# Attention beside a spectral filter: a clamped integer tile read directly as the first phase term, and the shifted copies of every second key block of VectorE made on GpSimd

## The chip, the cores and the metric

The kernel runs on one core of one Trainium2 chip. The time is device microseconds (us) of one launch; the times before are 455.18 and 456.29 us, median 455.74. The engines appear as PE (TensorE, matrix products; PEld is its weight load), ACT (ScalarE, activation functions), DVE (VectorE), POOL (GpSimd) and SP (its queue issues the DMAs here). SBUF is the on-chip memory, PSUM the memory that PE writes.

## The reference

Two branches over x of 2048 x 448 (bf16) are mixed by a gate for each row:

```python
g = sigmoid((x * gate_w).sum(-1, keepdims=True))
q, k, v = split(x @ wqkv)                 # 16 heads of 28
p = softmax(q @ k.T * 28 ** -0.5)         # 2048 x 2048 per head
a = concat(p @ v) @ wo
b = irfft2(rfft2(x) * (w_r + 1j * w_i))   # over both axes
out = g * a + (1 - g) * b
```

## The kernel before

**Attention.** Heads are worked in four groups g of four (index s), the queries in four blocks c of 512; a pair (g, c) is a *query group* n, 16 in all. Keys are cut in 16 blocks kt of 128. For one (n, kt, s), a *unit*, PE makes a 128 x 512 score tile. Most units are exponentiated by ACT: a *step* takes three units (PSUM tile psA) or two (psB) in turn, one activation at L1081 writes them to a ring in SBUF, and PE multiplies them with the values into the PSUM tile pvb (PV below). There are 363 steps.

**The key blocks of VectorE.** `ND` gives 29 (n, kt) blocks to DVE instead: key block 15 and key block 14 of n = 1 to 14, and block 15 of n = 15. I number them 0 to 28 in this order, so the blocks of kt = 15 are even and those of kt = 14 odd. For each, PE makes four score tiles (a "dunit" each, into one of two PSUM tiles bg0 and bg1). DVE turns each into a 16-bit integer that, read as a bf16, is a coarse power of two (L1040, "first pass", tile y4). Four shifted versions of that integer (phases f = 0 to 3) are made from it by four further DVE instructions of 128 x 2048 (L1050, tile pd), and PE adds the four in PV with weights vd that hold a gain for each phase (made on POOL at L951). The four together are a smoother exponential than one. The pd tiles go round a ring of NPD = 6, the y4 tiles a ring of two.

**Background.** Projections, the spectral branch (L1257 to L1389), normalisation (L1178 to L1193) and output tiles (L1214) use the same bg0 and bg1: PE fills one, DVE empties it.

**What sets the order.** `Sched.run` plans all work with assumed durations (0.61 us for a DVE pass, and so on), due times and dependencies, and emits each engine's instructions in the planned order; `pin` keeps that order. On the chip every engine runs its queue strictly in order and waits on semaphores for what its next instruction needs: data from another engine, or a tile that is still read. A wrong assumed duration is not corrected on the chip.

POOL otherwise makes memsets at the start, copies of weights, the vd tiles (L951) and sixteen small casts of softmax weights into the value tiles (L895).

Of the kernel before, what the change touches and what calls it, by code (L numbers as in the profile page):

```python
# [14 lines left out]
U16 = mybir.dt.uint16  # L15
ACT = mybir.ActivationFunctionType
ALU = mybir.AluOpType
# [3 lines left out]
NT, J, P = 16, 8, 128  # L21
FS, FN = (0, 112), 113
LN2 = math.log(2.0)
UNITS = 512.0
SQ = math.sqrt(UNITS * (DH ** -0.5) / LN2)
PHASE = (0, 129, 258, 387)
PHGAIN = [2.0 ** (-d / UNITS) / (4 * 1.0406815) for d in PHASE]
NPD, DKT = 6, 3


def free_dims(ap, dims, offset=0):
# [372 lines left out]
class Kernel:  # L404
# [28 lines left out]
    def alloc(self):  # L433
        nc, tc, ctx = self.nc, self.tc, self.ctx
        per = ctx.enter_context(tc.tile_pool(name="per", bufs=1))
        ps = ctx.enter_context(tc.tile_pool(name="ps", bufs=1, space=bass.MemoryType.PSUM))
        self.psA = ps.tile([P, 3, 512], F32, name="psA")
        self.psB = ps.tile([P, 2, 512], F32, name="psB")
        self.pv = ps.tile([P, 512], F32, name="pvb")
        self.bgt = [ps.tile([P, 512], F32, name=f"bg{i}") for i in range(2)]  # L440
        T = lambda shape, dt, name: per.tile(shape, dt, name=name)
        self.cst = T([P, CSTN], BF16, "cst")
        self.zero = T([P, 256], BF16, "zero")
        self.xtok = T([P, NT, 450], BF16, "xtok")
        self.xT = [T([P, 4, 512], BF16, f"xT{b}") for b in range(4)]
        self.wpad = {}
        for g in range(4):
            for w in "qk":
                self.wpad[w, g] = T([P, 4, P], BF16, f"wp{w}{g}") if g < 3 else self.wpad[w, 0]
        self.wv0 = T([P, 4, 112], BF16, "wv0")  # L450
        self.wvr = T([P, 4, 337], BF16, "wvr")
        self.WV0 = {1: 0, 2: 113, 3: 225}
        self.wo_pad = [T([P, D], BF16, f"wo{g}") for g in range(4)]
        self.q = [T([P, S], BF16, f"q{g}") for g in range(4)]
        self.k = [T([P, S], BF16, f"k{g}") for g in range(2)] * 2
        self.vw = [T([P, NT, 4, 32], BF16, f"vw{g}") for g in range(2)] * 2
        self.w = [T([P, NT, 4], F32, f"w{g}") for g in range(4)]
        self.ring = T([P, self.RING, 512], BF16, "ring")
        self.sq = T([P, S], BF16, "sq")
        self.nrow = [T([16, 512], BF16, f"nrow{i}") for i in range(2)]  # L460
        self.pvs = [T([P, 512], F32, f"pvs{i}") for i in range(2)]
        self.rs = [T([P, 16], F32, f"rs{i}") for i in range(2)]
        self.rr = [T([P, 16], F32, f"rr{i}") for i in range(2)]
        self.rhl = [T([P, 2, 16], BF16, f"rhl{i}") for i in range(2)]
        self.r8 = [T([8, 512], BF16, f"r8{i}") for i in range(2)]
        self.y4 = [T([P, 4, 512], U16, f"y4{i}") for i in range(2)]
        self.pd = [T([P, 4, 512], BF16, f"pd{i}") for i in range(NPD)]
        self.vd = T([P, 4, DKT, 4, 32], BF16, "vd")
        self.vf = T([P, DKT, 4, DH + 1], F32, "vf")
        self.glog = T([P, NT], F32, "glog")  # L470
        self.ge = T([P, NT], F32, "ge")
        self.gs = T([P, NT], F32, "gs")
        self.og = T([P, NT], F32, "og")
        self.Bd = T([P, 4, F2], BF16, "Bd")
        self.R = T([P, 4, 256], BF16, "R")
        self.Binv = self.Bd
        self.X1 = T([P, NT, F2], BF16, "X1")
        self.U = T([P, 2, 2, NT, 128], BF16, "U")
        self.CSt = [T([P, 3, P], BF16, f"CS{i}") for i in range(2)]
        self.Wg = [T([P, 3, F], BF16, f"Wg{i}") for i in range(2)]  # L480
        self.RBt = [T([P, 2, 2 * P], BF16, f"RB{i}") for i in range(2)]
        self.UT = [T([P, 2, F], BF16, f"UT{i}") for i in range(2)]
        self.t12 = [T([P, 2, F], BF16, f"t12{i}") for i in range(2)]
        self.t34 = [T([P, 2, F], BF16, f"t34{i}") for i in range(2)]
        self.ZT = [T([P, 2, 256], BF16, f"ZT{i}") for i in range(2)]
        self.bm = self.xtok
        self.fin = [T([P, D], BF16, f"fin{i}") for i in range(2)]

        self.wraw0 = {w: 2 * 4 * 336 + 448 * i for i, w in enumerate("qk")}
# [479 lines left out]
    def attention(self):  # L969
        nc, sc = self.nc, self.sc  # L970
# [5 lines left out]
        for b in range(4):  # L976
            due = ts[0] + 4 * b * rate
# [29 lines left out]
            el[-1:-1] = ph  # L1007
            self.elems.append(el)
        self.pdops, self.pv_last = {}, {}
        pdseq, quadl = [], []  # L1010
        di = 0
        dlist = [(n, kt) for n in range(16) for kt in self.dk[n]]
        for n, kt in dlist:
            g, c = self.groups[n]
            el = self.elems[n]
            fdue = []
            for f in range(4):
                i = el.index(("d", kt, f))
                t = self.tstart[n]
                for e in el[:i]:  # L1020
                    if e[0] == "a":
                        t = max(t, self.T[self.unit_step[n, e[1], 3]])
                fdue.append(t + 1.0)
            rel = fdue[0] - 60.0
            ys = self.y4[di % 2]
            prevy = quadl[di - 2][1][-1] if di >= 2 else None
            p1s = []
            for s in range(4):
                it = Item()

                def fm(s=s, g=g, c=c, kt=kt, it=it):
                    self.mm(self.bgi(it), self.k[g][32 * s:32 * s + 32, 128 * kt:128 * kt + 128],
                            self.q[g][32 * s:32 * s + 32, 512 * c:512 * c + 512], True, True, tile_position=(32 * s, 0))
                due = fdue[0] - DUE_P + 0.6 * s
                m = sc.op("PE", 0.22, fm, self.kev[g, kt // 4] + self.qev[g, c], due - 1, rel, "row", it, name="dunit")
                m.n = s
                self.dunit_ops.append(m)

                def f1(s=s, it=it, ys=ys):
                    self.pin(nc.vector.tensor_scalar(out=ys[:, s, :], in0=self.bgi(it), scalar1=127 * UNITS,  # L1040
                                                     scalar2=0.0, op0=ALU.add, op1=ALU.max))
                p1s.append(self.dve(0.61, f1, [m, prevy], due, free=it, name="dp1"))
            phs = []
            for f in range(4):
                j = len(pdseq)
                pds = self.pd[j % NPD]

                def g1(ys=ys, pds=pds, f=f):
                    fl = lambda t: t[:].rearrange("p a b -> p (a b)")
                    self.pin(nc.vector.tensor_scalar(out=fl(pds).bitcast(U16), in0=fl(ys), scalar1=float(PHASE[f]),  # L1050
                                                     scalar2=0.25, op0=ALU.add, op1=ALU.mult))
                o = self.dve(0.61, g1, p1s + phs[-1:], fdue[f], name="dexp")
                phs.append(o)
                pdseq.append((o, n, kt, f))
                self.pdops[n, kt, f] = (o, pds, j)
            quadl.append((p1s, phs))
            di += 1

# [4 lines left out]
        for i, st in enumerate(self.steps):  # L1063
            slot = self.psA if len(st) and i % 2 == 0 else self.psB
            deps = [exps[i - 2]] if i >= 2 else []
            for (n, kt, s) in st:
                g, c = self.groups[n]
# [8 lines left out]
            m = sc.op("PE", 0.23, fm, deps, -1000 + i * .001, 0.0, "row", name="score")  # L1076
# [6 lines left out]
            e = self.act(0.052 + 512 * len(st) / 1200.0, fe, [m] + exps[-1:], i * .001, name="exp")  # L1083
# [9 lines left out]
        pd_reader = {}  # L1093
# [3 lines left out]
        for n, (g, c) in enumerate(self.groups):  # L1097
            quads = self.elems[n]
            pairs = [quads[i:i + 2] for i in range(0, len(quads), 2)]
            for pi, pair in enumerate(pairs):  # L1100
                deps = [prev_pv]
# [3 lines left out]
                for kind, kt, *f in pair:  # L1105
                    deps += self.vready[g, kt // 4]
                    if kind == "a":
                        for s in range(4):
                            deps.append(unit_exp[n, kt, s])
                        tk = max(tk, self.T[self.unit_step[n, kt, 3]])  # L1110
                    else:
                        deps += [self.pdops[n, kt, f[0]][0], self.vdready[g]]

                def fm(pair=pair, pi=pi, n=n, g=g, last=(pi == len(pairs) - 1)):
                    for qi, (kind, kt, *f) in enumerate(pair):
# [8 lines left out]
                o = self.pe(0, fm, deps, tk + 2.0, mode="col", name="pv", dur=0.225 * len(pair))  # L1124
# [13 lines left out]
        for e in exps:  # L1138
            for ug in e.n:
                r = unit_reader.get(ug - self.RING)  # L1140
                if r is not None:
                    e.deps.append(r)
        for o, pds, j in self.pdops.values():
            if j >= NPD:
                o.deps.append(pd_reader[j - NPD])
        for g in range(1, 4):
            for o in self.vdops[g]:
                o.deps.append(self.vdlast.get(g - 1))
# [1 line left out]
        kr = {g: [] for g in range(4)}  # L1150
# [2 lines left out]
                for u in self.steps[o.step]:  # L1153
                    kr[self.groups[u[0]][0]].append(o)
        for (n, kt, f), (o, pds, j) in self.pdops.items():
            kr[self.groups[n][0]][-1:-1] = [o]
        last_s = {g: kr[g][-1] for g in range(4)}
        for o in sc.ops:
            nd = []
# [280 lines left out]
```

## Time and profile before

| row | us | of the span | instructions |
|---|---|---|---|
| profiled execution, span | 455.7 | | 9292 |
| PE | 416.1 | 91% | 3661 |
| ACT | 416.9 | 91% | 386 |
| DVE | 327.9 | 72% | 621 |
| POOL | 39.5 | 9% | 75 |

The profiled execution's span is 455.7 us from its first to its last instruction. Its share of an engine is the time in which at least one of that engine's instructions was in progress. Groups of instructions are listed by source line, with the written tile, the read tile, partitions x elements, count, summed time and the mean of one in ns. The sums of ACT's two groups exceed ACT's busy time because successive activations overlap in the records; rates are therefore read from start to start.

### The profile page before, as it was taken

The page shows a single profiled execution, that of the slowest core. Times are in us where ns is not written, and L with a number is a line of the kernel's source. Part 1 is how long each engine was busy: PE and PEld are TensorE (multiplying, and loading weights), DVE is VectorE, ACT ScalarE, POOL GpSimd, SP SyncE. Part 2 cuts the span into 40 slices and gives each one's busy share as a digit, 9 for nine tenths or more (in the row PEclk, how much of TensorE's full clock was granted, in tenths as well). Part 3 has the DMA queues.
Part 4 walks back from the last instruction along what each step waited for, and adds up shares of the span by engine and source line. Part 5 has one row for each costly group of instructions (what it writes and reads, how often), then busy time and mean ns, then how long its engine had stood idle before and what let it go on. Part 6 is the DMA issues. An engine that isn't in the chain of part 4 may idle for free.

```text
span 455.7 us, 9292 instructions
## 1 busy us (share of the span) xinstructions
PE 416.1 (91%) x3661; PEld 164.9 (36%) x3678; DVE 327.9 (72%) x621; ACT 416.9 (91%) x386; POOL 39.5 (9%) x75
## 2 busy tenths in 40 slices
PE   7799999999999889899998998999999999998895
PEld 4344222333443333234433332234443333323353
DVE  3355876978759989996798887886667787892213
ACT  1488999998999999999999999999999999999960
POOL 7401300000013000000040000000013000000000
PEclk9799999999999999999999999999999899999999
DMA  8202010101101222201120010000001000100101
GB/s 246 35 0 66 3 36 2 44 0 35 20 4 27 57 41 49 51 11 44 26 50 3 0 27 2 14 24 15 14 14 38 23 25 24 33 21 23 42 1 42
DMA packets 28364, 14.03 MB, mean 31 GB/s; under 512 B 18176, under 2 KB 27936, under 8 KB 28320
## 3 DMA queue, kind: packets, MB, share of 16 engines
q1 hardware_dynamic: 27216, 13.09, 11.6%
q8 instruction: 28, 0.46, 0.4%
q10 hardware_dynamic: 1104, 0.35, 0.4%
q14 instruction: 16, 0.13, 0.1%
HBM read 11.21 MB, written 1.84 MB: 29 GB/s over the span
## 4 chain that ended last, share of the span: by engine, by line
ACT 48%; PE 28%; issue 12%; DVE 7%; DMA 3%; SPq 1%; ACTq 0%; DVEq 0%
ACT ring L1081 48%; PE bg L518 11%; PE pvb L518 6%; PE psA L518 5%; PE psB L518 4%; PE bg L521 2%; DVE pd L1050 1%; DVE y L1040 1%; DMA U<-in_A_wqkv_dram 1%; DMA r<-rhl 1%; DMA rs<-pvs 1%; DVE U L1282 1%; SPq L500 1%; ACT w L890 0%; DVE pvs L1178 0%
## 5 line engine op out<-in xcount | busy, mean ns | idle before, releaser
L1081 ACT ACTIVATE ring<-psA 128x1536 bf16<-128x1536 f32 x182 | 294.2, 1616 | 6.9 <-PE psA L518 5.1
L1081 ACT ACTIVATE ring<-psB 128x1024 bf16<-128x1024 f32 x181 | 216.2, 1194 | 1.2 <-PE pvb L518 1.1
L1040 DVE TENSOR_SCALAR y<-bg 128x512 uint16<-128x512 f32 x116 | 78.9, 686 | 24.1 <-PE bg L518 23.3
L518 PEld LDWEIGHTS <-k 32*128 32x128 bf16 x1024 | 46.9, 91 | 127.6 <-issue 115.8
L518 PE MATMUL psA<-q,k 32*128 32x512 bf16 x546 | 72.2, 383 | 19.7 <-ACT ring L1081 15.4
L518 PE MATMUL pvb<-ring,vw 128*32 128x512 bf16 x908 | 80.6, 385 | 0.1
L1050 DVE TENSOR_SCALAR pd<-y 128x2048 uint16<-128x2048 uint16 x116 | 79.1, 697 | 0.8 <-PE pvb L518 0.2
L518 PE MATMUL psB<-q,k 32*128 32x512 bf16 x362 | 71.9, 384 | 2.8 <-ACT ring L1081 1.7
L518 PE MATMUL pvb<-pd,vd 128*32 128x512 bf16 x464 | 46.3, 386 | 0.1
L518 PE MATMUL bg<-q,k 32*128 32x512 bf16 x116 | 43.3, 384 | 2.2 <-DVE X L1257 0.9
L518 PEld LDWEIGHTS <-vw 128*32 128x32 bf16 x908 | 19.5, 94 | 24.8 <-issue 20.7
L895 POOL CAST vw<-w 128x16 bf16<-128x16 f32 x16 | 4.2, 262 | 257.6 <-ACT w L890 257.6
L1282 DVE CAST U<-bg 113x512 bf16<-113x512 f32 x32 | 21.6, 683 | 6.6 <-PE bg L518 6.4
L518 PE MATMUL bg<-R,X 128*113 128x256 bf16 x128 | 24.0, 287 | 0.7 <-DVE U L1282 0.4
L518 PEld LDWEIGHTS <-xT 128*128 128x128 bf16 x320 | 18.5, 97 | 14.0 <-issue 12.1
L1178 DVE COPY pvs<-pvb 128x512 f32<-128x512 f32 x16 | 11.0, 684 | 14.9 <-PE pvb L518 14.8
L951 POOL TENSOR_SCALAR vd<-vf 128x348 bf16<-128x348 f32 x16 | 19.8, 1238 | 17.0 <-DVE vf L940 16.0
L1214 DVE SCALAR_TENSOR_TENSOR fin<-bg,gs,xtok 128x448 bf16<-128x448 f32 x16 | 10.9, 681 | 12.0 <-PE bg L518 11.9
L518 PE MATMUL bg<-Bd,ZT 113*128 113x448 bf16 x64 | 17.8, 356 | 0.2 <-DVE ZT L1376 0.2
L518 PEld LDWEIGHTS <-zero 128*128 128x128 bf16 x154 | 14.6, 104 | 9.2 <-issue 5.5
L518 PEld LDWEIGHTS <-X 128*113 128x113 bf16 x128 | 13.1, 130 | 12.5 <-issue 12.4
L518 PE MATMUL bg<-xT,wpk 128*128 128x512 bf16 (+1 forms) x52 | 16.5, 383 | 1.1 <-issue 0.6
(96 smaller groups left out, 419.4 us busy)
## 6 DMA issues: line engine op xcount, KB each, us to landing
RB<-cRB SPq DMA_DIRECT2D x16, 128.0 KB
Wg<-in_B_w_i_dram SPq DMA_DIRECT2D x32, 56.2 KB
xtok<-in_A_x_dram SPq DMA_DIRECT2D x4, 448.0 KB
out_dram<-fin SPq DMA_DIRECT2D x16, 112.0 KB
CS<-cCS SPq DMA_DIRECT2D x16, 96.0 KB
Wg<-in_B_w_r_dram SPq DMA_DIRECT2D x16, 56.2 KB
r<-rhl SPq DMA_DIRECT2D x32, 4.0 KB
U<-in_A_wqkv_dram SPq DMA_DIRECT2D x2, 252.0 KB
```

Of the source, the lines that this page charges most:

```text
L500: self.pin(e.dma_start(out=out() if callable(out) else out, in_=in_() if callable(in_) else in_))
L518: self.pin(self.nc.tensor.matmul(out, lhsT=lhsT, rhs=rhs, start=start, stop=stop, **kw))
L521: self.pin(self.nc.tensor.transpose(out=out, in_=in_, identity=self.c("ident")[0:n, 0:n]))
L895: self.pin(nc.gpsimd.tensor_copy(out=free_dims(self.vw[g][:], [[128, 4], [32, 4]], 4 * b * 128 + DH), in_=self.w[g][:, 4 * b:4 * b + 4, :]))
L951: self.pin(nc.gpsimd.tensor_scalar(out=self.vd[:, f, :, :, 0:DH + 1], in0=self.vf[:], scalar1=PHGAIN[f], scalar2=None, op0=ALU.mult))
L1040: self.pin(nc.vector.tensor_scalar(out=ys[:, s, :], in0=self.bgi(it), scalar1=127 * UNITS, scalar2=0.0, op0=ALU.add, op1=ALU.max))
L1050: self.pin(nc.vector.tensor_scalar(out=fl(pds).bitcast(U16), in0=fl(ys), scalar1=float(PHASE[f]), scalar2=0.25, op0=ALU.add, op1=ALU.mult))
L1081: self.pin(nc.scalar.activation(out=self.ring[:, u0:u0 + len(st), :], in_=slot[:, 0:len(st), :], func=ACT.Exp, scale=LN2 / UNITS))
L1178: ev = self.dve(0.61, lambda: self.pin(nc.vector.tensor_copy(out=pvs[:], in_=self.pv[:])), [last, self.nlast[i]], -100.0)
L1214: self.pin(nc.vector.scalar_tensor_tensor(out=fin[:], in0=self.bgi(it)[:, 0:D], scalar=self.gs[:, t:t + 1], in1=self.bm[:, t, 0:D], op0=AL ...
L1282: self.pin(nc.vector.tensor_copy(out=dst, in_=src))
```

## The change

The integer that the first pass makes is now in units of 1/128 of a power of two instead of 1/512, so that it is a finished bf16 bit pattern, clamped at zero. It is written straight into the pd tile of phase 0; the tile y4 is gone. The shifts become 0, 32, 64 and 96 and the factor of the shifted copies 1.0. Three copies (f = 1 to 3) remain for each block. Those of the even blocks (di even) stay on DVE, those of the odd blocks go to POOL, where the planner assumes 1.85 us for one and a due time 2 us earlier. The ring of pd tiles grows to 8, so that even blocks always use pd0 to pd3 and odd ones pd4 to pd7. The planner's dependency of a first pass on the last shifted copy two blocks back is gone; it now knows one on PV's read of the tile that is overwritten. The semaphore waits for tiles that are read and overwritten are derived from the accesses themselves, beside the planner.

```diff
-UNITS = 512.0
+UNITS = 128.0
-PHASE = (0, 129, 258, 387)
+PHASE = (0, 32, 64, 96)
-NPD, DKT = 6, 3
+NPD, DKT = 8, 3
+PHENG = [("DVE", "DVE", "DVE"), ("POOL", "POOL", "POOL")]
...
-        self.y4 = [T([P, 4, 512], U16, f"y4{i}") for i in range(2)]
...
-            ys = self.y4[di % 2]
-            prevy = quadl[di - 2][1][-1] if di >= 2 else None
+            j0 = 4 * di
+            ys = self.pd[j0 % NPD]
...
                 def f1(s=s, it=it, ys=ys):
-                    self.pin(nc.vector.tensor_scalar(out=ys[:, s, :], in0=self.bgi(it), scalar1=127 * UNITS,
-                                                     scalar2=0.0, op0=ALU.add, op1=ALU.max))
-                p1s.append(self.dve(0.61, f1, [m, prevy], due, free=it, name="dp1"))
+                    self.pin(nc.vector.tensor_scalar(out=ys[:, s, :].bitcast(U16), in0=self.bgi(it),
+                                                     scalar1=127 * UNITS, scalar2=0.0, op0=ALU.add, op1=ALU.max))
+                p1s.append(self.dve(0.61, f1, [m], due, free=it, name="dp1"))
             phs = []
-            for f in range(4):
-                j = len(pdseq)
-                pds = self.pd[j % NPD]
-
-                def g1(ys=ys, pds=pds, f=f):
-                    fl = lambda t: t[:].rearrange("p a b -> p (a b)")
-                    self.pin(nc.vector.tensor_scalar(out=fl(pds).bitcast(U16), in0=fl(ys), scalar1=float(PHASE[f]),
-                                                     scalar2=0.25, op0=ALU.add, op1=ALU.mult))
-                o = self.dve(0.61, g1, p1s + phs[-1:], fdue[f], name="dexp")
+            self.pdops[n, kt, 0] = (p1s, ys, j0)
+            for f in range(1, 4):
+                pds = self.pd[(j0 + f) % NPD]
+                eng = PHENG[di % len(PHENG)][f - 1]
+
+                def g1(ys=ys, pds=pds, f=f, eng=eng):
+                    fl = lambda t: t[:].rearrange("p a b -> p (a b)").bitcast(U16)
+                    e = nc.vector if eng == "DVE" else nc.gpsimd
+                    self.pin(e.tensor_scalar(out=fl(pds), in0=fl(ys), scalar1=float(PHASE[f]),
+                                             scalar2=1.0, op0=ALU.add, op1=ALU.mult))
+                o = sc.op(eng, 0.61 if eng == "DVE" else 1.85, g1, p1s, fdue[f] - (2.0 if eng == "POOL" else 0.0),
+                          name="dexp")
                 phs.append(o)
...
-                        deps += [self.pdops[n, kt, f[0]][0], self.vdready[g]]
+                        deps += self.pdops[n, kt, f[0]][0] + [self.vdready[g]]
```

More of the change, by code (lines that the diff above doesn't have):

```diff
@@ L1009, in attention @@
         self.pdops, self.pv_last = {}, {}
-        pdseq, quadl = [], []
+        quadl = []
         di = 0
@@ L1039, in f1 @@
                 def f1(s=s, it=it, ys=ys):
-                    self.pin(nc.vector.tensor_scalar(out=ys[:, s, :], in0=self.bgi(it), scalar1=127 * UNITS,
-                                                     scalar2=0.0, op0=ALU.add, op1=ALU.max))
-                p1s.append(self.dve(0.61, f1, [m, prevy], due, free=it, name="dp1"))
+                    self.pin(nc.vector.tensor_scalar(out=ys[:, s, :].bitcast(U16), in0=self.bgi(it),
+                                                     scalar1=127 * UNITS, scalar2=0.0, op0=ALU.add, op1=ALU.max))
+                p1s.append(self.dve(0.61, f1, [m], due, free=it, name="dp1"))
             phs = []
-            for f in range(4):
-                j = len(pdseq)
-                pds = self.pd[j % NPD]
-                def g1(ys=ys, pds=pds, f=f):
-                    fl = lambda t: t[:].rearrange("p a b -> p (a b)")
-                    self.pin(nc.vector.tensor_scalar(out=fl(pds).bitcast(U16), in0=fl(ys), scalar1=float(PHASE[f]),
-                                                     scalar2=0.25, op0=ALU.add, op1=ALU.mult))
-                o = self.dve(0.61, g1, p1s + phs[-1:], fdue[f], name="dexp")
+            self.pdops[n, kt, 0] = (p1s, ys, j0)
[9 more added lines that the diff above has]
+                          name="dexp")
                 phs.append(o)
-                pdseq.append((o, n, kt, f))
-                self.pdops[n, kt, f] = (o, pds, j)
+                self.pdops[n, kt, f] = ([o], pds, j0 + f)
             quadl.append((p1s, phs))
@@ L1142, in attention @@
                     e.deps.append(r)
-        for o, pds, j in self.pdops.values():
+        for ops, pds, j in self.pdops.values():
             if j >= NPD:
-                o.deps.append(pd_reader[j - NPD])
+                for o in ops:
+                    o.deps.append(pd_reader[j - NPD])
         for g in range(1, 4):
@@ L1155, in attention @@
         for (n, kt, f), (o, pds, j) in self.pdops.items():
-            kr[self.groups[n][0]][-1:-1] = [o]
+            kr[self.groups[n][0]][-1:-1] = o
         last_s = {g: kr[g][-1] for g in range(4)}
```

## The prediction

> **What bounds the kernel now.** I read the page's busy shares first, then its chain of waits, then busy time by stretch, and last the costliest groups.
>
> ```profile
> PE 416.1 (91%) x3661; PEld 164.9 (36%) x3678; DVE 327.9 (72%) x621; ACT 416.9 (91%) x386; POOL 39.5 (9%) x75
> ...
> ACT 48%; PE 28%; issue 12%; DVE 7%; DMA 3%; SPq 1%; ACTq 0%; DVEq 0%
> ...
> L1040 DVE TENSOR_SCALAR y<-bg 128x512 uint16<-128x512 f32 x116 | 78.9, 686 | 24.1 <-PE bg L518 23.3
> ...
> L1050 DVE TENSOR_SCALAR pd<-y 128x2048 uint16<-128x2048 uint16 x116 | 79.1, 697 | 0.8 <-PE pvb L518 0.2
> ```
>
> ACT carries 48% of the chain, DVE 7%. DVE's two passes cost 79 us each, and the first (L1040) waits for PE, not PE for it. The stretches (us; then PE, PEld, DVE, ACT and POOL busy time with counts, clock, DMA) show where ACT is not full:
>
> ```profile
> 22.00:50.00 28.00, 26.76 (x250) 11.78 (x251) 16.11 (x29) 25.42 (x26) 4.02 (x10) 1.00 0.09 27
> 50.00:135.00 85.00, 80.07 (x686) 29.42 (x690) 65.91 (x120) 81.56 (x77) 3.77 (x9) 1.00 0.08 19
> 135.00:230.00 95.00, 86.00 (x827) 32.21 (x832) 85.47 (x180) 95.00 (x90) 7.59 (x10) 1.00 0.17 37
> 230.00:340.00 110.00, 101.47 (x931) 40.33 (x932) 85.83 (x160) 109.98 (x102) 4.98 (x10) 1.00 0.07 17
> 340.00:440.00 100.00, 94.14 (x803) 34.78 (x802) 62.88 (x113) 98.18 (x87) 5.25 (x4) 0.98 0.09 26
> ```
>
> From 22 to 440 us ACT is idle 2.6 + 3.4 + 0 + 0 + 1.8 = 7.8 us. So between start and tail ACT is the bound, also from 135 to 230 us, where DVE is 90% busy. DVE can have any spare time there: it gives back 7.8 us at the most (1.7%). ACT's own work is unchanged.
>
> The timeline gives ACT's pace (start, duration):
>
> ```profile
> 137.27 1.60 ACT L1081 ACTIVATE ring<-psA 128x1536 bf16<-128x1536 f32 x1
> ...
> 139.53 1.60 ACT L1081 ACTIVATE ring<-psA 128x1536 bf16<-128x1536 f32 x1
> ```
>
> Two steps take 139.53 - 137.27 = 2.26 us; over a longer run the chain shows 2.24, so a step is 1.12 us. I use it as a clock for the order of the changed kernel.
>
> **What goes from DVE.** Of 116 shifted copies 29 (f = 0) vanish, 42 (three for each of 14 odd blocks) move to POOL, 45 stay. 71 x 0.697 = 49.5 us less DVE time, to 278 us. The first pass keeps its 116 instructions of 0.686 us; only its destination changes. Since ACT does not wait for DVE, I credit 1 us of the 7.8: the waits for a pd tile in the profile are about that (PEld for pd: 1.1 us). Constants, 8 instead of 6 tiles and a few filler matmuls less: nothing, the same instructions on the same path.
>
> **What a copy costs on POOL.** No row has it. Three POOL forms bound it: two copies from the list of groups (each shape apart), and from the answer for the tile vd the operation that is moved.
>
> ```profile
> L608 POOL COPY wpk<-U 128x336 bf16<-128x336 bf16 x3 | 1.4, 466 | 6.7 <-PE bg L518 3.5 <-DMA U<-in_A_wqkv_dram 3.1
> ...
> L611 POOL COPY wpk<-U 64x112 bf16<-64x112 bf16 x3 | 0.8, 278 | 0.0
> ```
>
> ```profile
> L951 POOL TENSOR_SCALAR vd<-vf x16: 1082/1084/1666, 47.5 to 344.4; 128x348 bf16<-128x348 f32 x16
> ```
>
> The two copies differ by 188 ns for 224 elements: 0.84 ns each and 0.18 us fixed. At that rate 2048 elements take 1.9 us. A TENSOR_SCALAR, the operation that is moved, has 348 elements and takes 1.084 us undisturbed (the last line: minimum, median, maximum). With the same fixed 0.18 us that is 2.59 ns an element, so 2048 take 5.5 us. If instead all of its excess over a copy were fixed, 0.79 us, the price is 2.5 us. Upwards: the moved form has two arithmetic operations where L951 has one; were the second as dear as the first (2.59 - 0.84 = 1.75 ns), it is 9.1 us. I take 5.5 us, the row of the same operation by its slope, and keep 1.9 to 9.1. The planner assumes 1.85.
>
> [...]
>
> **Where the longer copy lands.** POOL itself has room: 39.5 + 42 x 5.5 = 271 us. But the three copies of an odd block run one after the other, and two things wait for them. PV's reads of f = 1 to 3 do; and, new, the next odd block's first pass on DVE, since it overwrites pd4, which the three copies still read. The queue order of the changed kernel shows that wait: the first L1040 of each odd block from block 3 on waits for POOL. Behind it in DVE's queue stand the evacuations of bg0 and bg1, for these PE, and for PE's scores ACT.
>
> I count steps in PE's queue. L is the step of an odd block's last dunit, D that of the next odd block's first. D - L for blocks 1, 3, 5, ... 25: 12, 7, 30, 5, 10, 10, 13, 14, 11, 12, 14, 9, 16. For block 27, with no successor, the last read (f = 3) comes at L + 12. The reads are late by less than the first pass wherever both are late, except there and at single steps, so I count each block once.
>
> At T per copy, the third ends at L + 1 + 3T/1.12 (1 step for the first pass of the last tile). For T = 5.5 that is L + 15.7. DVE is held for 15.7 - (D - L) where positive: 3.7, 8.7, 0, 10.7, 5.7, 5.7, 2.7, 1.7, 4.7, 3.7, 1.7, 6.7, 0, and 3.7 for block 27.
>
> Not all of it reaches ACT. In the queue order at block 5, the first dunit fills bg0 at step 66 and the next use of bg0 is at step 68; until then PE needs nothing from DVE. I therefore take two steps off each: 1.7 + 6.7 + 8.7 + 3.7 + 3.7 + 0.7 + 2.7 + 1.7 + 4.7 + 1.7 = 36 steps, 40 us. With no cover it would be 59 steps, 66 us. ACT is full before and after each stall, so nothing is caught up.
>
> The small POOL work queued among the copies (L895, L951) may run up to 16 us later. In the queue order group 2's first two casts stand ahead of block 13's copies, and the others ahead of the PV steps that read their key blocks: zero, at worst one further triple of a few us per group change (three changes); I leave that to the range.
>
> Sum, against the profiled execution: 455.7 + 40 - 1 = 494.7 us. The span and the median (455.74) agree within 0.1 us, so no correction.
>
> **The rivals.** *(B) POOL copies at the rate of its COPY rows (1.9 to 2.5 us): not slower.* The third copy then ends at L + 6.1 to L + 7.7. Only D - L = 5 and 7 are below: 1.2 us at 1.9, 3.8 us at 2.5 without cover, 0.8 with it. With 0 to 4 us of the 7.8 gained: 452 to 459 us. It decides up to about T = 3.5, where the sum with cover is 5.4 us, without 12. For it: COPY and MEMSET on POOL; the fixed part of L951 is not known. Against: the L951 row by its slope.
>
> *(C) POOL's copies also hold up DVE's own SBUF copies.* At the start a DVE copy beside a POOL memset shows it:
>
> ```profile
> 6.01 1.91 POOL L747 MEMSET vw<- 128x2048 bf16 x1
> 6.09 1.87 DVE L611 COPY wpk<-U 64x112 bf16<-64x112 bf16 x1
> ...
> 139.20 1.35 POOL L951 TENSOR_SCALAR vd<-vf 128x348 bf16<-128x348 f32 x1
> 139.29 0.93 DVE L1050 TENSOR_SCALAR pd<-y 128x2048 uint16<-128x2048 uint16 x1
> ```
>
> The DVE copy, 0.58 us in its other row, ends with the memset. But L1050 under a POOL TENSOR_SCALAR takes 0.93 instead of 0.68 us and ends at 140.22, before POOL's 140.55. At that price 45 copies lose at most 45 x 0.25 = 11 us, inside the 49.5 us that DVE gained: nothing. If they waited out POOL's whole triple, the even blocks whose first pass ends inside one while the next odd block has not yet arrived (after blocks 15, 17, 19, 25 and 27: 2, 2, 4, 5.5 and 10.5 steps) add 24 steps, 27 us: 522 us. [...]
>
> *(D) The change doesn't do what it says.* The planner could have kept the copies apart from their use; it has not, and POOL's queue holds all 42.
>
> **How the numbers follow.** POOL at 4.5 to 6 us a copy, as forecast: 0.43; own range 472 (T = 4.5 with cover, 16 us) to 522 (T = 5.5 without cover). C: 0.10, about 522. B: 0.30, 452 to 459. Between (2.6 to 4.4 us): 0.10, 458 to 472, a third of it above 465. Dearer copies (6.8 us: 88 us, 9.1: 177): 0.05, 543 to 632. A gain of most of the 7.8 us and of tail work: 0.02. 2% of 455.7 is 9 us, about what a measurement of this kernel can tell from no change. Slower by more: 0.43 + 0.10 + 0.05 + 0.03 = 0.61. Within: 0.30 + 0.07 = 0.37. Faster: 0.02. The range takes in B, the middle and the forecast's own: 451 to 523, about 0.87; leaving B out would drop too much.
>
> **What would show it.** In the profile after: POOL's L1052 group of 42 near 5.5 us (B: near 2); POOL busy near 270 us; DVE's L1040 with idle time ended by POOL, some tens of us, where now PE ends it; ACT's idle between 22 us and the tail near 47 us; DVE's L1052 group, 45, near 0.7 to 1.0 us (C: well above 2). The forecast is wrong if POOL's copy is below 3.5 us, or if PE runs on past the held DVE for much longer than two steps.

## The result, and the profile after

The changed kernel takes 477.58 us (476.59 to 478.58, two runs) against 455.74: a ratio of 1.048, 95% interval 1.037 to 1.059. It is slower, inside the range that was forecast and on the side that was forecast. The reason that the forecast gave is not the one that the trace shows. Some executions run up to 3% longer at a lower clock (of one version 471.8 us at 0.953 beside 457.9 at 0.989); the ratios here leave these out, so that a ratio can differ a little from the quotient of the two medians.

The page of the changed kernel: engines, chain, then the groups that answer to those shown of before.

```profile
span 476.0 us, 9311 instructions
PE 430.7 (90%) x3673; PEld 165.2 (35%) x3673; DVE 306.5 (64%) x550; ACT 419.8 (88%) x386; POOL 116.1 (24%) x117
...
ACT 39%; PE 34%; issue 12%; DVE 10%; DMA 3%; SPq 1%; ACTq 0%; DVEq 0%
...
L1052 POOL TENSOR_SCALAR pd<-pd 128x2048 uint16<-128x2048 uint16 x42 | 79.6, 1917 | 196.6 <-DVE pd L1040 77.8
L1040 DVE TENSOR_SCALAR pd<-bg 128x512 uint16<-128x512 f32 x116 | 78.4, 686 | 35.6 <-PE bg L518 34.0
...
L1052 DVE TENSOR_SCALAR pd<-pd 128x2048 uint16<-128x2048 uint16 x45 | 30.0, 689 | 0.3
```

A POOL copy takes 1.9 us, not the 5.5 of the forecast. DVE's first pass (L1040) waits for PE, and no wait for POOL is listed. DVE's own copies are as long as before (689 ns, 697 before). So neither a dear copy nor a late one costs the time. Yet ACT, which lost 7.8 us between 22 and 440 us, now loses 23.5 there (stretch, PE, PEld, DVE, ACT, POOL busy time with counts, clock, DMA):

```profile
50.00:135.00 85.00, 79.47 (x643) 27.12 (x635) 58.72 (x98) 79.79 (x73) 20.84 (x17) 0.96 0.08 19
135.00:230.00 95.00, 85.55 (x735) 28.91 (x732) 75.99 (x149) 83.83 (x78) 22.22 (x17) 0.91 0.15 34
230.00:340.00 110.00, 98.99 (x887) 37.36 (x884) 80.45 (x142) 105.45 (x97) 33.23 (x23) 0.97 0.07 17
```

From 135 to 230 us ACT was full before; now it loses 11 us, and PE's granted clock is 0.91 where it was 1.00. The timelines of POOL, DVE, PE and ACT at one of the odd blocks show what happens there (start, duration, instruction, idle time before it and what ended it):

```profile
196.90 5.64 POOL L1052 TENSOR_SCALAR pd<-pd 128x2048 uint16<-128x2048 uint16 x3 [17.31 <-PE psA L518]
```

```profile
199.09 1.70 DVE L1347 TENSOR_TENSOR X<-t 128x225 bf16<-128x225 bf16 x1
200.71 1.96 DVE L1351 TENSOR_TENSOR X<-t 128x225 bf16<-128x225 bf16 x1
202.59 0.24 DVE L1185 RECIPROCAL rr<-rs 128x16 f32<-128x16 f32 x1
```

```profile
200.99 0.39 PE L518 MATMUL psA<-q,k 32*128 32x512 bf16 x3
...
201.54 0.39 PE L518 MATMUL pvb<-ring,vw 128*32 128x512 bf16 x4
203.90 0.38 PE L518 MATMUL bg<-sq,cst 128*16 128x512 bf16 x1 [1.97 <-DVE pd L1040]
...
206.44 0.61 PE L518 MATMUL psA<-q,k 32*128 32x512 bf16 x3
```

```profile
201.59 1.61 ACT L1083 ACTIVATE ring<-psA 128x1536 bf16<-128x1536 f32 x1
204.70 1.02 ACT L1083 ACTIVATE ring<-psB 128x1024 bf16<-128x1024 f32 x1 [1.50 <-PE psB L518]
207.16 1.45 ACT L1083 ACTIVATE ring<-psA 128x1536 bf16<-128x1536 f32 x1 [1.44 <-PE psA L518]
```

Three POOL copies run from 196.90 to 202.54. Two DVE instructions of 0.27 us each (both read two SBUF tiles) take 1.70 and 1.96 us meanwhile; the second ends just after POOL does. DVE's queue stands behind them, PE idles 1.97 us for it. The three matmuls into psA, 0.39 us before, then take 0.61: the granted clock is 0.50 from 206 to 214 us, and ACT waits for scores several times.

I call the time by which a DVE instruction is longer than undisturbed, while POOL works beside it, a *hold*. Holds sum to 18.5 us on DVE, in 19 instructions: two-input instructions in SBUF (L1347, L1351, L840, L1187) and a copy of 16 elements within SBUF (L1186), the longest taking 1.97 us. DVE's copies L1052 have 0.17 us of it, and 0.6 us lie beside L951, not beside a copy. Set the start of each ACT step beside that of before, and the lag grows by 2.4, 2.5, 1.9, 6.2 and 4.8 us around the copies at 112, 156, 174, 197 and 303 us, 17.8 us in all; the last step is 19.2 us later. The rest is not still: the lag also grows by 1.9 us near 92 us and by 2.8 us between 135 and 144 us, where no hold lies, and it falls by 1.9 us near 110 us and by 2.1 us between 380 and 389 us.

### The profile page after: what moved, and what is told of

It reads as the page before. It is cut to its first block, busy times and chain, and to the rows that moved or that the text cites. A ratio compares the mean times of both kernels' runs of the same rounds, so it can differ in the third digit from the quotient of the medians.

```text
span 476.0 us, 9311 instructions
## 1 busy us (share of the span) xinstructions
PE 430.7 (90%) x3673; PEld 165.2 (35%) x3673; DVE 306.5 (64%) x550; ACT 419.8 (88%) x386; POOL 116.1 (24%) x117
## 4 chain that ended last, share of the span: by engine, by line
ACT 39%; PE 34%; issue 12%; DVE 10%; DMA 3%; SPq 1%; ACTq 0%; DVEq 0%
ACT ring L1083 38%; PE bg L518 13%; PE pvb L518 8%; PE psA L518 6%; PE psB L518 5%; PE bg L521 2%; DMA r<-rhl 1%; DVE pd L1040 1%; DVE X L1351 1%; DMA U<-in_A_wqkv_dram 1%; SPq L500 1%; DVE rhl L1187 1%; DMA rs<-pvs 1%; DVE t L1341 1%; DVE rhl L1186 1%
## 5 line engine op out<-in xcount | busy, mean ns | idle before, releaser
L1083 ACT ACTIVATE ring<-psA 128x1536 bf16<-128x1536 f32 x182 | 288.5, 1585 | 14.9 <-PE psA L518 13.1
L1083 ACT ACTIVATE ring<-psB 128x1024 bf16<-128x1024 f32 x181 | 209.5, 1157 | 8.9 <-PE bg L518 6.1
L1052 POOL TENSOR_SCALAR pd<-pd 128x2048 uint16<-128x2048 uint16 x42 | 79.6, 1917 | 196.6 <-DVE pd L1040 77.8
L1040 DVE TENSOR_SCALAR pd<-bg 128x512 uint16<-128x512 f32 x116 | 78.4, 686 | 35.6 <-PE bg L518 34.0
L518 PE MATMUL pvb<-ring,vw 128*32 128x512 bf16 x908 | 82.6, 395 | 0.1
L518 PE MATMUL psB<-q,k 32*128 32x512 bf16 x362 | 73.4, 391 | 2.3 <-ACT ring L1083 1.2
L518 PE MATMUL pvb<-pd,vd 128*32 128x512 bf16 x464 | 47.9, 401 | 0.0
L1052 DVE TENSOR_SCALAR pd<-pd 128x2048 uint16<-128x2048 uint16 x45 | 30.0, 689 | 0.3
L951 POOL TENSOR_SCALAR vd<-vf 128x348 bf16<-128x348 f32 x16 | 17.3, 1081 | 15.2 <-DVE vf L940 8.4
L518 PE MATMUL bg<-xT,wpq 128*128 128x512 bf16 (+1 forms) x60 | 19.0, 397 | 0.0
L518 PE MATMUL bg<-xT,wpk 128*128 128x512 bf16 (+1 forms) x60 | 17.8, 387 | 0.5 <-DVE xT L801 0.3
```

What stands on the lines that cost most here:

```text
L518: self.pin(self.nc.tensor.matmul(out, lhsT=lhsT, rhs=rhs, start=start, stop=stop, **kw))
L951: self.pin(nc.gpsimd.tensor_scalar(out=self.vd[:, f, :, :, 0:DH + 1], in0=self.vf[:], scalar1=PHGAIN[f], scalar2=None, op0=ALU.mult))
L1040: self.pin(nc.vector.tensor_scalar(out=ys[:, s, :].bitcast(U16), in0=self.bgi(it), scalar1=127 * UNITS, scalar2=0.0, op0=ALU.add, op1=ALU. ...
L1052: self.pin(e.tensor_scalar(out=fl(pds), in0=fl(ys), scalar1=float(PHASE[f]), scalar2=1.0, op0=ALU.add, op1=ALU.mult))
L1083: self.pin(nc.scalar.activation(out=self.ring[:, u0:u0 + len(st), :], in_=slot[:, 0:len(st), :], func=ACT.Exp, scale=LN2 / UNITS))
```

## The experiments

**Order or copies?** Every queue keeps its order and every wait; from the second odd block on, POOL copies 8 of 2048 columns (the other shifted values are left out).

```diff
+w = 8 if eng == "POOL" and di > 1 else 2048
-e.tensor_scalar(out=fl(pds), in0=fl(ys), ...)
+e.tensor_scalar(out=fl(pds)[:, 0:w], in0=fl(ys)[:, 0:w], ...)
```

> The 39 POOL copies after the first odd block handle 8 of their 2048 columns (the rest of the shifted values is left out); every queue keeps the order of the changed kernel, and every wait stays. Theory H (hold): a POOL copy that is running holds up DVE instructions that read two SBUF tiles or copy within SBUF until it ends, PE then starves for DVE and its granted clock falls; with short copies no hold: 455 to 460 us, L1347, L1351, L840 and L1187 all near their undisturbed 0.27, 0.27, 0.42 and 0.17 us, clock near 0.98. Rival O (order): the newly planned queue order costs the time by itself: 474 to 478 us, clock near 0.96.

454.59 us against 459.58 of the kernel before on that chip, ratio 0.989 (0.984 to 0.994). No clock below 0.97 shows between 20 us and the tail, and the holds sum to 0.6 us, all beside L951. The new queue order costs nothing; it is even faster without long POOL copies. The order as a cause falls.

**Shorter instructions.** Each POOL copy in four instructions of 512 columns.

```diff
+w = 2048 if eng == "DVE" else 512
+for a in range(0, 2048, w):
+    e.tensor_scalar(out=fl(pds)[:, a:a + w], in0=fl(ys)[:, a:a + w], ...)
```

> Each POOL copy is made as four instructions of 512 columns, all else as in the changed kernel. Theory H: one hold lasts as long as one POOL instruction, so at most about 0.6 us instead of 1.97; the 18.5 us by which DVE's instructions were longer become about 5: 457 to 463 us. Rival L (latency): what costs is that the copies come late for PV and for the next first pass; four instructions have a longer total (about 2.4 us for a copy by the COPY rows), so 477 us or more. Rival O: 474 to 478 us.

462.5 us, ratio 1.004 (1.000 to 1.008). The copies take longer in all (168 x 641 ns, 103 us summed against 79.6), and the kernel is faster than the changed one: lateness of the copies is not the cause. The longest extension of a two-input instruction is now 0.48 us, the sum about 10 us in 28 holds, more than the 5 I expected.

**The other half of the change.** All copies on DVE, planned anew:

```diff
-PHENG = [("DVE", "DVE", "DVE"), ("POOL", "POOL", "POOL")]
+PHENG = [("DVE", "DVE", "DVE")]
```

> All shifted copies on DVE, planned anew; the clamped first phase and the eight pd tiles stay. Theory H: POOL holds nothing up, DVE has 29 copies (20 us) less than before, ACT bounds: 452 to 457 us. Rival: the other half of the change (first phase without a copy, ring of 8) costs by itself: above 465 us.

Ratio 0.999 (0.994 to 1.005). The clamped first phase and the ring of eight cost nothing; the 29 copies less of DVE gain nothing that can be seen.

**Reading or writing?** POOL's copies become memsets, which write as long and read nothing (the shifted values are left out).

```diff
+if eng == "POOL" and di > 1:
+    e.memset(pds[:].rearrange("p a b -> p (a b)"), 0.5)
```

> The 39 POOL copies after the first odd block become memsets of the same tile, so POOL writes SBUF for as long (about 1.8 us) but reads nothing (the shifted values are left out); order as in the changed kernel. If any POOL instruction holds DVE up: L1347, L1351, L840 still reach 1.9 us, 472 to 478 us. If for the two-input instructions it is POOL's reading that counts: these stay at 0.27 to 0.43 us, only copies within SBUF (L1186, L1052) are longer, 456 to 466 us.

501.35 us, ratio 1.092 (1.085 to 1.100): my time was wrong, since I had not expected the copies within SBUF to suffer so much. The two kinds of DVE instruction do part ways. DVE's groups and two places in the timelines of POOL and DVE:

```profile
L1055 DVE TENSOR_SCALAR pd<-pd 128x2048 uint16<-128x2048 uint16 x45 | 51.8, 1174 | 0.3
L1189 DVE CAST rhl<-rr 128x16 bf16<-128x16 f32 x16 | 13.1, 818 | 0.3
...
L1350 DVE TENSOR_TENSOR X<-t 128x225 bf16<-128x225 bf16 x16 | 4.5, 287 | 0.0
L1354 DVE TENSOR_TENSOR X<-t 128x225 bf16<-128x225 bf16 x16 | 4.2, 268 | 0.0
L1190 DVE TENSOR_TENSOR rhl<-rr,rhl 128x16 bf16<-128x16 f32 x16 | 2.8, 174 | 0.5
```

```profile
288.92 4.09 POOL L1053 MEMSET pd<- 128x2048 bf16 x2 [24.46 <-PE pvb L518]
```

```profile
289.04 0.42 DVE L840 TENSOR_TENSOR sq<-k 128x512 bf16<-128x512 bf16 x1
289.37 1.90 DVE L1055 TENSOR_SCALAR pd<-pd 128x2048 uint16<-128x2048 uint16 x1
```

```profile
380.79 2.24 POOL L951 TENSOR_SCALAR vd<-vf 128x348 bf16<-128x348 f32 x2
382.97 5.29 POOL L1053 MEMSET pd<- 128x2048 bf16 x3
```

```profile
382.58 5.71 DVE L1189 CAST rhl<-rr 128x16 bf16<-128x16 f32 x1
```

The two-input instructions are back at 287, 268 and 174 ns. The means alone would not show much, since L1190 met no memset; but seven two-input instructions ran beside one, in part or whole, four of them begun after it, and none was more than 0.01 us longer than undisturbed. At 289.04 us L840 takes its 0.42 us while the copy behind it, under the same memset, takes 1.90 instead of 0.68. So in these runs it is POOL's *reading* that holds two-input instructions (they took up to 1.97 us beside a copy, at most 0.01 us longer than undisturbed beside a memset). Copies within SBUF are held by POOL's writing too (1.90 us instead of 0.68), and one of 16 elements waits out the end of an L951 and three memsets in a row, 5.71 us. The memsets also wait for less (not for the first pass), start earlier, and so meet DVE's copies, which POOL's copies had hardly met.

**Plan around it.** The planner keeps those DVE instructions (named sb2, and DVE's copies) off the time in which it has a POOL copy running or ready; a copy is planned at 1.9 us. A filler matmul after a group's last PV is left out, which by itself does not alter any queue of the changed kernel.

```diff
+shut = e == "DVE" and (t < held_until[0] + 0.3 or any(
+    p.name == "dexp" and rdy[p] <= t + 0.3 for p in pend["POOL"]))
...
+if shut and o.name in ("sb2", "dexp"):
+    continue
```

> The planner starts no DVE instruction that reads two SBUF tiles (L840, L1187, the two that write X) or copies within SBUF (L1186, L1052 on DVE) while it has a POOL copy running or ready; the copy is planned at 1.9 us, and a filler matmul after the last PV of a group is left out. The POOL copies stay whole. Theory H: these instructions wait in the plan instead of at the head of DVE's queue, the sum by which they are longer falls from 18.5 us to below 6, and the time to 450 to 458 us, as with the short copies (ratio 0.985 to 1.0). If the delay only moves to what waits for these instructions: 465 us or more.

> The plan that keeps DVE's instructions within SBUF off the POOL copies, once more: 0.985 to 0.996 of the kernel before.

454.71 us on one chip, ratio 0.991 (0.986 to 0.996); 457.15 us on another, ratio 0.993 (0.988 to 0.997). Its POOL and DVE groups:

```profile
L1059 POOL TENSOR_SCALAR pd<-pd 128x2048 uint16<-128x2048 uint16 x42 | 78.7, 1897 | 168.1 <-DVE pd L1047 110.5 <-PE bg L525 29.5 <-DVE rr L1192 15.9
...
L1354 DVE TENSOR_TENSOR X<-t 128x225 bf16<-128x225 bf16 x16 | 4.4, 286 | 0.0
L1358 DVE TENSOR_TENSOR X<-t 128x225 bf16<-128x225 bf16 x16 | 4.1, 267 | 0.0
```

The 42 whole copies are all there, the holds sum to 1.5 us in four instructions, and the version is faster than both kernels. With the same plan and copies in quarters:

> As the run before, and each POOL copy in four instructions of 512 columns (planned at 2.35 us). Theory H: what still collides waits 0.6 us instead of 1.9; 450 to 458 us, at or up to 3 us below the whole copies with the same plan. If the shorter hold no longer matters once the plan avoids it: the same within 1%.

the runs lay between 457.9 and 471.8 us and allow no ratio: inconclusive. Its profile has fifteen holds with about 5 us. And all copies on DVE beside the planned version:

> All copies on DVE, once more, beside the run before on one chip: 0.99 to 1.005. If freeing DVE by POOL gains anything, the run before is faster than this one; if ACT's pace bounds both, they agree within 0.5%.

1.006 (1.002 to 1.010), a little above my range, against 0.993: with POOL's help and hardly anything held the kernel is about 1% faster than with DVE alone (the two plans differ in other places too).

**The changed kernel again, on one chip with the planned version.**

> The changed kernel itself, for a ratio on the same chip as the others: 1.037 to 1.059 against the kernel before.

471.18 us, ratio 1.026 (1.020 to 1.032), below my expectation. Its profile has the same holds, 18.3 us in 18 instructions, but a span of 467.2 instead of 476.0 us. The time missing from a full clock, summed over stretches of 2 us, is 6.8 us where the first had 15.3. So 8.8 us of span go with 8.5 us of clock at equal holds: a good part of the loss is time at half of the clock, and how much of it there is varies. In the first profile five of six stretches at half clock before the last step start within 3 us after a hold ends. The sixth, 3.4 us at 92 us, comes before the first hold; the kernel before has one such stretch, too, at 358 us, and the version with all copies on DVE, in its second run, two of 3.4 us, at 91 and 115 us. So holds set off most of these stretches, as far as their place tells, but not all.

**The price of a copy.** Two kernels with spare POOL instructions, all phase copies on DVE and a ring of six (their own times are not read).

> All shifted copies on DVE with a ring of six pd tiles, and three rounds of six POOL instructions on spare tiles between 150 and 230 us, to find why the POOL TENSOR_SCALAR of L951 takes 1.08 us for 348 elements when the copy of 2048 takes 1.9: 348 f32 to bf16, flat; 348 bf16 to bf16, flat; 348 bf16 into 12 rows of 29 with a stride of 32; 2048 bf16 flat with one operation; a plain copy of 2048 bf16; and L951's own form. By the 12 short rows: the two in rows take 1.0 to 1.1 us, the flat ones 0.45 to 0.5. By the f32 input: the two with f32 take 1.0 to 1.1. By a fixed part of one-operation TENSOR_SCALAR: all of 348 take 1.0 to 1.1 and the 2048 takes 2.5.

All forms of 348 elements took 1.07 to 1.10 us undisturbed, whatever type or layout, so rows and f32 fall; but 2048 with one operation took 5.37 us or more, not 2.5, so a fixed part falls as well. The plain copy took 1.89 to 2.22. What was left is the number of operations:

> As the first probe, with other forms on POOL: 2048 bf16 with one and with two operations, 2048 uint16 with one and with two, and L951's form (348 f32 into 12 rows of 29) with two and with one. If the number of operations decides: 5.4 us and 1.9 us for either type, and L951's form with two operations 0.45 to 0.5 instead of 1.08 us. If the type decides: bf16 5.4 us both times, uint16 1.9 both times, L951's form 1.08 both times.

From the timeline of POOL, where L1007 and L1009 have one operation on 2048 elements, L1008 and L1010 two, L1011 has L951's form with two and L1012 with one:

```profile
165.50 5.36 POOL L1007 TENSOR_SCALAR pr<-pr 128x2048 bf16<-128x2048 bf16 x1
170.94 1.90 POOL L1008 TENSOR_SCALAR pr<-pr 128x2048 bf16<-128x2048 bf16 x1
...
243.58 5.38 POOL L1009 TENSOR_SCALAR pr<-pr 128x2048 uint16<-128x2048 uint16 x1
249.04 1.90 POOL L1010 TENSOR_SCALAR pr<-pr 128x2048 uint16<-128x2048 uint16 x1
...
258.69 0.48 POOL L1011 TENSOR_SCALAR prs<-pr 128x348 bf16<-128x348 f32 x1
259.26 1.08 POOL L1012 TENSOR_SCALAR prs<-pr 128x348 bf16<-128x348 f32 x1
```

With two operations on 2048 elements POOL is 2.8 times as fast as with one, for either type (1.90 us against 5.36 and 5.38).

**The forecast's own price.** POOL's copies with the addition alone, so that they cost what the forecast assumed:

```diff
-e.tensor_scalar(out=fl(pds), in0=fl(ys), scalar1=..., scalar2=1.0, op0=ALU.add, op1=ALU.mult)
+e.tensor_scalar(out=fl(pds), in0=fl(ys), scalar1=..., scalar2=None, op0=ALU.add)
```

> The POOL copies have one operation (add) instead of two (add, times 1.0); same values, same queue order. By the probe (one-operation TENSOR_SCALAR of 2048 at 5.4 us or more) each copy takes about 5.5 us, and the recorded sum for that price applies: DVE's first pass waits for POOL, 494 us, and more by the holds, which last up to 5.5 us: 494 to 530 us. If the 1.9 us come from the integer type and not from the second operation, the copy stays at 1.9 us and the time at the changed kernel's (1.02 to 1.05 of before).

562.27 us, ratio 1.222 (1.212 to 1.233), above my range. The groups of POOL's copies and DVE's first pass:

```profile
L1056 POOL TENSOR_SCALAR pd<-pd 128x2048 uint16<-128x2048 uint16 x42 | 226.1, 5405 | 166.5 <-DVE pd L1040 86.4 <-DVE rhl L1191 24.4 <-PE pvb L518 19.0
L1040 DVE TENSOR_SCALAR pd<-bg 128x512 uint16<-128x512 f32 x116 | 78.6, 686 | 69.6 <-PE bg L518 38.9 <-POOL pd L1056 29.4 <-PE psB L518 0.6
```

At 5.4 us the wait that the forecast described does appear, 29.4 us of it. On top come 66 us of holds and 63 us missing from a full clock, which the recorded sum of 40 us had not. The three overlap and do not add up to the loss.

## Why the prediction came out as it did

**What bounds the kernel** was read rightly: ACT, with 7.8 us to win at most. Full copies with hardly any holds won about 1% against the kernel before, more than the 1 us credited, and within that bound.

**DVE's saving** of 49.5 us was right for the copies: 79.1 to 30.0 us. But 18.5 us returned as holds. Its busy time, in which overlapping records count once, fell by 21 us only.

**The price of the copy** is the step that failed: 5.5 us forecast, 1.9 measured. By the forecast's own sign, a copy below 3.5 us, it is wrong. The slope from L951 was right for its form, since one operation on 2048 elements takes 5.4 us. The step "Upwards: ... were the second as dear as the first" took it for granted that a second operation costs something. With the second operation the probe's instruction was 2.8 times as fast, 1.90 us against 5.36. The 1.9 us by the rate of the COPY rows, which the forecast set aside for L951's row, was close; that row could not speak against it, having one operation.

**Where the longer copy lands** therefore did not happen: at 1.9 us no first pass waited for POOL. At the assumed price the wait is real, but the sum was too small, because it left out holds and clock.

**Rival B** had the price right and the time wrong (452 to 459 us): with copies at 1.9 us it counted lateness alone. With holds removed by the plan, 0.991 and 0.993 of before are what it describes.

**Rival C** had the mechanism and the wrong victim. It asked what POOL does to DVE's own copies and found 11 us inside DVE's gain: "nothing". These copies lost 0.17 us, because only two of the 45 met a POOL copy. The price of 0.25 us a meeting, read from a pair beside L951, does not hold in general: beside the one-operation copies a DVE copy took up to 5.84 us. Why the meetings with L951 cost so little (0.24 to 0.31 us in all six of the profile of before) stays open. The victims were the other instructions in SBUF, first the two-input ones, which the profile of before lists and which the forecast never set beside POOL's new work. And it charged a hold at DVE's spare time, where the place decides: two holds of 3 us together stopped PE, and with the clock at half behind them ACT lost 6 us.

That the direction and the range held is luck: they rested on the case that fell, and the right answer, a cheap copy and a slower kernel, had no case of its own.

## What to carry to other kernels

Before moving work to POOL, list every DVE instruction that reads two SBUF tiles or copies within SBUF, not just those of the step that moves, and see which of them fall in POOL's new time: in these traces such an instruction stood at the head of DVE's queue until the POOL copy beside it was done, for up to 1.97 us, and one for 5.71 us beside the end of an L951 and three memsets. A planner that knew this kept the gain (0.991 and 0.993 of before), and shorter POOL instructions limited the loss (1.004 in quarters, against 1.048 and 1.026). Take an engine's price from the same operation in the same form, down to the number of its operations (5.36 us with one, 1.90 with two).

## What the runs showed of the hardware that was not expected

A TENSOR_SCALAR of 128 x 2048 on POOL takes 5.36 us with one operation and 1.90 us with two when undisturbed; in the changed kernel the one that starts at 258.21 us, 0.09 us after a DVE copy within SBUF of 0.69 us, took 2.36 us, so that there POOL was held too. For 348 elements it takes 1.08 and 0.48 us. By my estimate from these two, L951 could be had for less than half by a factor of 1.0 as a second operation; that was not tried in the kernel itself. A DVE cast of 16 elements, 0.17 us alone, took 5.71 us beside the end of an L951 and three POOL memsets in a row. A PE gap of 1.97 us, to 203.90 us, was followed by some 10 us at half of the clock, from 204.5 us on.
